# Expert units: the order of passes in the first part; first FFN group: the first product as three rounded products

## The chip, the cores and the metric

The kernel runs on one core of one Trainium2 chip. The metric is the device time of one execution in microseconds (us); the time of a kernel is the median of its runs. Engines are named as the profile names them: PE (TensorE matmul; PEld its weight loads), DVE (VectorE), ACT (ScalarE), POOL (GpSimd), SP (SyncE, whose queue issues most DMAs).

## What is computed

Three stages on 2304 tokens of width 512. A linear attention with 4 batches and 8 heads, an FFN with a softplus between its two products, and a routed layer in which each token goes to one of 8 experts:

```python
# attention: phi(x) = exp(x omega^T - |x|^2/2 - max) / sqrt(m)
num = einsum('bhsm,bhmd->bhsd', q_p, einsum('bhsm,bhsd->bhmd', k_p, v))
x = (num / (einsum('bhsm,bhm->bhs', q_p, k_p.sum(2)) + 1e-6))   # -> [2304, 512]
# FFN, d_ff = 2048
h = x @ w_in
x = (maximum(h, 0) + log1p(exp(-abs(h)))) @ w_out
# routed layer, 8 experts of hidden size 1024, one expert for each token
out[mask] = gate_w[mask, None] * (maximum(x[mask] @ w1[e], 0) @ w2[e])
```

The FFN's weights come from the host as 64-bit floats and are turned into 32-bit ones on the chip.

## The kernel before

**Formats of a product.** A product of two 32-bit operands is done in one of two ways. Plain: one matmul of type F32 for each block of 128 rows of the contraction; the profile shows it as two records on PE. Rounded: each operand is split into a high part (a copy rounded to the type F32R, `..h` or `..hi`) and a rest (the operand minus its high part, `..l` or `..lo`, F32R too); then three matmuls are summed: high by high, high by rest, rest by high. A split costs a cast (ACT, mostly) and a subtraction (DVE or POOL) for each operand.

**Attention** is cut into small steps (`stage_T`, `P`, `K`, `Z`, `Q`, `N`, `M`, `X`): transposes, projections (three matmuls `pp`, L282 to L284), the sums over keys (`kv`), the numerators and denominators (`nd`), and the division (`stage_M`, L425 and L426 on POOL, then a DVE operation at L433). `stage_X` splits the result into `xhi` (L252) and `xlo` (L444, on POOL). Of the first group of tokens it leaves out the split: L433 writes the plain tile `x` there.

**FFN.** Tokens go in 6 groups of 384 (`NG`), the hidden width in 16 chunks of 128 (`NF`). Chunk f of a group makes `h` (`mm1`, 128 by 384, contraction 512 in four blocks), the softplus (`r`, `t`, `gf` or `gh` and `gl`), and adds to the output sums `y` (`mm2`, L703). In group 0 both products are plain: four F32 matmuls on the chunk's weights `win` in `mm1` and three in `mm2`. In groups 1 to 5 they are rounded: `ring_in` casts the chunk's weights to `wih` (ACT, L597) and subtracts the rest `wil` (L598, DVE or POOL by the table `il`, in which the entries of group 0 are both POOL), in two buffers each, one chunk ahead.

During group 0 the FFN's weights are loaded and converted: 32 pieces (`w_in` and `w_out` of 16 chunks) pass through three staging buffers `wst`; SP issues the load, and three DVE operations make 32-bit floats of a piece (L558, L561, L564), after which its staging buffer is free for the next load.

The attention steps of later tokens are laid between the FFN's matmuls. Up to the first expert unit a scheduler sets the order of instructions on each engine; each engine then runs its own list in order.

**Expert units.** A unit is one block of 128 tokens of one expert (single, `slot_*`) or two (pair, `pair_*`). Four singles come first, then six times a pair and a single, then a last single. In these units, from the second on, the written order is kept. For each unit 2 MB of `w1` and 2 MB of `w2` are gathered by POOL's DMAs, cast on ACT (`w`, L1246) and their rests taken on DVE (L1250), `w1` in four blocks c = 0 to 3 while PE works on the unit ahead. The unit's first product is made in two parts (single, L1336, twelve matmuls of 128x512 each) or four (pair, L1358, 24 of 128x256 each). In each part the passes of one block stand together:

```python
PASSES = ((0, 0), (0, 1), (1, 0))        # (part of x, part of w1): 0 high, 1 rest
mms = [(xs[g][a][c], w1s[g, c][b_][:, w]) for c in range(NC) for a, b_ in PASSES]
```

Of the kernel before, what the change touches and what calls it, by code (L numbers as in the profile page):

```python
# [9 lines left out]
F32 = mybir.dt.float32  # L10
# [5 lines left out]
ALU = mybir.AluOpType  # L16
# [60 lines left out]
def tile_kernel(ctx, tc, q, k, v, omega, w_in, w_out, emb, tau, w1, w2, out):  # L77
# [156 lines left out]
    def x_tiles(g):  # L234
        if g == 0:

            xg[g] = xg.get(g) or [xpool.tile([P, NC, G], F32, tag="xhi", name="x_0"), None]
        elif g not in xg:
            xg[g] = [xpool.tile([P, NC, G], F32R, tag=f"x{s}", name=f"x{s}_{g}") for s in ("hi", "lo")]
        return xg[g]  # L240
# [174 lines left out]
    def stage_M(b, u, i, half):  # L415
# [10 lines left out]
        nc.gpsimd.tensor_tensor(out=den, in0=den, in1=rc, op=ALU.mult)  # L426

        parts = [(slice(0, HW[half]), xf)]
        if b == 0:
            parts = [(slice(o, o + n), x_tiles(0)[0][:, 2 * u + i, off:off + n] if g == 0 else xf[:, o:o + n])  # L430
                     for g, off, o, n in x_pieces(b, half)]
        for c, out_ in parts:
            nc.vector.scalar_tensor_tensor(out=out_, in0=den[:, c], scalar=2.0, in1=xf[:, c], op0=ALU.subtract,  # L433
                                           op1=ALU.mult, reverse0=True)

    def stage_X(b, u, i, half):
        den, xf = st.pop(("x", b, u, i, half))
        j = 2 * u + i
        for g, off, done, n in x_pieces(b, half):
            if g == 0:  # L440
                continue
            xh, xl = x_tiles(g)
            move("xh", b, u, xh[:, j, off:off + n], xf[:, done:done + n])
            eng("xl", b, u).tensor_tensor(out=xl[:, j, off:off + n], in0=xf[:, done:done + n],  # L444
                                          in1=xh[:, j, off:off + n].bitcast(F32), op=ALU.subtract)
# [135 lines left out]
    def conv_to(n):  # L581
        while done_w[0] < min(n, NW):
            next(conv, None)
# [5 lines left out]
    def ring_in(n):  # L589
        f = n % NF  # L590
        if n < NF:
            return
        assert done_w[0] >= 2 * f + 1
        ih = ring.tile([P, NC, P], F32R, tag="wih", name="wih")
# [26 lines left out]
    def mm1(n, rate):  # L621
        g, f = divmod(n, NF)
        xh, xl = xg[g]
        if g == 0:
            conv_to(2 * f + 1)
            passes = ((win_chunk(f), xh),)
        else:
            ih, il = wr.pop(("i", n))
            passes = ((ih, xh), (il, xh), (ih, xl))

# [25 lines left out]
        else:  # L656
            nc.vector.scalar_tensor_tensor(out=t, in0=r, scalar=2.0, in1=h[:, 0:G], op0=ALU.mult, op1=ALU.subtract)  # L657
        if n + 1 < NG * NF and n >= 1:
            ring_in(n + 1)
# [609 lines left out]
    PASSES = ((0, 0), (0, 1), (1, 0))  # L1269

    def unit_x(g):

# [55 lines left out]
    def slot_m1(g, half, part=slice(0, 12)):  # L1328
# [3 lines left out]
        w = slice(half * HF, half * HF + HF)  # L1332
        mms = [(xs[g][a][c], w1s[g, c][b_][:, w]) for c in range(NC) for a, b_ in PASSES]
        for i in range(part.start, part.stop):
# [16 lines left out]
    def pair_m1(g, k):  # L1351

        ph = hs["ps"] = mpsum("h", "ph")
        for c in range(NC):
            for j in range(2):
                f = slice(2 * k * P + j, 2 * (k + 1) * P, 2)
                for n, (a, b_) in enumerate(PASSES):
                    nc.tensor.matmul(ph[:, j * 256:j * 256 + 256], lhsT=w1s[g, c][b_][:, f],  # L1358
                                     rhs=xs[g][a][c].rearrange("p i t -> p (i t)"),
                                     start=(c == 0 and n == 0 and j == 0), stop=(c == NC - 1 and n == 2),  # L1360
                                     skip_group_check=True)

# [227 lines left out]
```

## Time and profile before

| | us |
|---|---|
| median of 3 runs | 950.11 (948.86 to 951.63) |
| the profiled execution's own time | 950.99 |
| its span, first to last instruction | 949.1 |
| PE busy over the span | 895.0 (94%) |
| DVE, ACT, POOL busy | 694.6, 651.7, 345.1 |
| granted TensorE clock, mean | 0.991 of full |

PE is busy nearly throughout, so the first thing to read is where it is not, and what its work costs from the start of one matmul to the start of the next: records of neighbouring matmuls overlap, so a group's mean duration is longer than what it takes of PE. The first 150 us, in which loads, conversions and attention share the engines with group 0, have to be read apart from the rest.

### The profile page before, as it was taken

What the parts mean: (1) busy time and instruction counts of PE and PEld (TensorE: products, weight loads), DVE (VectorE), ACT (ScalarE), POOL (GpSimd) and SP (SyncE); (2) the same over time, 40 slices, a digit from 0 to 9 for tenths busy, and PEclk for the clock granted to TensorE, in tenths of its full rate; (3) what the DMA queues carried; (4) which work ended last, traced back from release to release, by engine and by line L of the source; (5) the groups of instructions that cost most, each with busy time, mean ns of one, the idle gap of its engine ahead of it and who ended that gap; (6) DMA issues with size and microseconds to landing.
All of it is one profiled execution on the core that took longest, in us unless ns stands there. A gap on an engine that the chain in (4) does not pass through costs nothing. (4 is left out here: it accounts for less than half of the span.)

```text
span 949.1 us, 14505 instructions
## 1 busy us (share of the span) xinstructions
PE 895.0 (94%) x4951; PEld 743.6 (78%) x4951; DVE 694.6 (73%) x1376; ACT 651.7 (69%) x1452; POOL 345.1 (36%) x341
## 2 busy tenths in 40 slices
PE   7788989999999999999999999999999999999993
PEld 6666545588888879887888889887787887878872
DVE  6698875477888776689886777768967676685762
ACT  4787445477778867776777678876867576585672
POOL 1332400255446654566653110012653242252410
PEclk9999999999999999999999999999999999999997
DMA  4656660011262212010301281102114661451820
GB/s 117 188 170 199 185 180 28 12 39 37 56 147 69 48 47 71 26 40 17 67 7 23 73 331 63 34 12 57 34 56 161 253 240 70 169 211 36 324 86 6
DMA packets 86540, 94.69 MB, mean 100 GB/s; under 512 B 50294, under 2 KB 74870, under 8 KB 84160
## 3 DMA queue, kind: packets, MB, share of 16 engines
q1 hardware_dynamic: 77888, 45.21, 18.4%
q0 software_dynamic: 8576, 48.52, 13.7%
q8 instruction: 41, 0.67, 0.3%
q14 instruction: 35, 0.29, 0.1%
HBM read 108.36 MB, written 15.48 MB: 130 GB/s over the span
## 5 line engine op out<-in xcount | busy, mean ns | idle before, releaser
L1370 PE MATMUL po<-w,mh_h 128*128 128x512 f32 x368 | 116.8, 398 | 0.5 <-ACT mh_h L1347 0.5
L1385 POOL DMA_INDIRECT out_dram<-ot,s_idx x23 | 46.3, 2015 | 166.9 <-ACT ot L1384 126.0
L703 PE MATMUL y<-woh,gh 128*128 128x512 f32 x240 | 97.7, 411 | 3.2 <-DVE gh L682 3.2
L1250 DVE TENSOR_TENSOR w<-w2r,w 128x512 fp32r<-128x512 f32 x136 | 88.2, 687 | 12.3 <-ACT w L1246 12.1
L703 PE MATMUL y<-wol,gh 128*128 128x512 f32 x240 | 94.9, 398 | 0.0
L1246 ACT CAST w<-w2r 128x512 fp32r<-128x512 f32 x136 | 79.4, 643 | 18.4 <-DMA w2r<-in_moe_w_dram,w_idx 9.0
L1250 DVE TENSOR_TENSOR w<-w1r,w 128x1024 fp32r<-128x1024 f32 x68 | 80.3, 1226 | 11.2 <-ACT w L1246 11.2
L703 PE MATMUL y<-woh,gl 128*128 128x512 f32 x240 | 81.5, 406 | 0.4 <-POOL gl L683 0.4
L598 DVE TENSOR_TENSOR wil<-win,wih 128x512 fp32r<-128x512 f32 x72 | 56.9, 790 | 29.2 <-ACT wih L597 25.9
L638 PE MATMUL h<-xhi,wih 128*128 128x384 f32 x320 | 73.6, 349 | 2.8 <-DVE t L657 2.5
L1370 PEld LDWEIGHTS po<-w,mh_h 128*128 128x128 f32 x368 | 66.1, 189 | 12.2 <-ACT mh_h L1347 0.7
L1246 ACT CAST w<-w1r 128x1024 fp32r<-128x1024 f32 x68 | 71.9, 1121 | 3.8 <-PE ph L1336 2.1
L1358 PE MATMUL ph<-mxh,w 128*128 128x256 f32 x384 | 73.0, 286 | 1.4 <-DVE w L1250 0.5
L1370 PE MATMUL po<-w,mh_l 128*128 128x512 f32 x184 | 72.6, 395 | 1.7 <-DVE mh_l L1349 1.7
L425 POOL TENSOR_TENSOR xf<-xf,rc 128x256 f32<-128x256 f32 (+1 forms) x20 | 19.9, 994 | 143.7 <-ACT rc L424 129.0
L638 PE MATMUL h<-xlo,wih 128*128 128x384 f32 x320 | 71.9, 340 | 0.0
L638 PE MATMUL h<-xhi,wil 128*128 128x384 f32 x320 | 69.6, 337 | 0.0
L1358 PEld LDWEIGHTS ph<-mxh,w 128*128 128x128 f32 x384 | 62.7, 195 | 5.1 <-DVE w L1250 3.8
L610 POOL TENSOR_TENSOR wol<-wout,woh 128x512 fp32r<-128x512 f32 x40 | 54.2, 1355 | 27.8 <-ACT woh L609 24.9
L638 PEld LDWEIGHTS h<-xhi,wih 128*128 128x128 f32 x320 | 55.1, 188 | 7.6 <-DVE t L657 3.0
L638 PEld LDWEIGHTS h<-xhi,wil 128*128 128x128 f32 x320 | 57.5, 188 | 0.0
L638 PEld LDWEIGHTS h<-xlo,wih 128*128 128x128 f32 x320 | 56.5, 188 | 0.5
(311 smaller groups left out, 2415.1 us busy)
## 6 DMA issues: line engine op xcount, KB each, us to landing
wst<-in_moe_w_in_dram SPq DMA_DIRECT2D x16, 512.0 KB, 3.9
wst<-in_moe_w_out_dram SPq DMA_DIRECT2D x16, 512.0 KB, 3.7
raw<-in_k_dram SPq DMA_DIRECT2D x32, 128.0 KB, 2.3
vf<-in_v_dram SPq DMA_DIRECT2D x64, 64.0 KB, 2.2
raw<-in_q_dram SPq DMA_DIRECT2D x32, 128.0 KB, 2.3
ya<-yt SPq DMA_DIRECT2D x20, 128.2 KB, 3.9
yb<-yt SPq DMA_DIRECT2D x20, 128.2 KB, 3.6
ya<-yt SPq DMA_DIRECT2D x8, 256.5 KB, 4.7
```

The lines of the kernel that those rows point to most:

```text
L425: nc.gpsimd.tensor_tensor(out=xf, in0=xf, in1=rc, op=ALU.mult)
L598: feng("il", n).tensor_tensor(out=il, in0=wi, in1=ih.bitcast(F32), op=ALU.subtract)
L610: feng("ol", n).tensor_tensor(out=ol, in0=wo, in1=oh.bitcast(F32), op=ALU.subtract)
L638: nc.tensor.matmul(h[:, 0:G], lhsT=a[:, c, :], rhs=x[:, c, :], start=(i == 0), stop=(i == last))
L703: nc.tensor.matmul(y, lhsT=x[:, c], rhs=w, start=(f == 0 and i == 0), stop=(f == NF - 1 and i == len(passes) - 1))
L1246: nc.scalar.copy(out=hi, in_=src)
L1250: eng.tensor_tensor(out=lo, in0=src, in1=hi.bitcast(F32), op=ALU.subtract)
L1358: nc.tensor.matmul(ph[:, j * 256:j * 256 + 256], lhsT=w1s[g, c][b_][:, f], rhs=xs[g][a][c].rearrange("p i t -> p (i t)"), start=(c == 0 an ...
L1370: nc.tensor.matmul(po[s], lhsT=h[a][:, o:o + P], rhs=w2s[g, c][b_], start=(c == 0 and n == 0), stop=(c == 7 and n == 2))
L1385: nc.gpsimd.indirect_dma_start(out=out, out_offset=bass.IndirectOffsetOnAxis(ap=s_idx[:, s:s + 1].bitcast(U32), axis=0), in_=ot, in_offset ...
```

## The change

In group 0 the first product `mm1` is made rounded, as in the other groups: `x` of group 0 is split like the others' (`xhi`, `xlo`), `ring_in` runs for its 16 chunks too, and the single F32 pass over four blocks becomes three F32R passes. The order of the three passes in every group's `mm1` becomes high by high, weights' high by `x`'s rest, weights' rest by `x`'s high. `stage_M` writes its result with one DVE operation instead of one for each piece. In an expert unit's first part the matmuls with `w1`'s rests come after all the others (`first_order`); in a pair's parts the two halves j now alternate inside each pass.

```diff
--- before.py
+++ after.py
@@ -232,10 +232,7 @@
     xg = {}
 
     def x_tiles(g):
-        if g == 0:
-
-            xg[g] = xg.get(g) or [xpool.tile([P, NC, G], F32, tag="xhi", name="x_0"), None]
-        elif g not in xg:
+        if g not in xg:
             xg[g] = [xpool.tile([P, NC, G], F32R, tag=f"x{s}", name=f"x{s}_{g}") for s in ("hi", "lo")]
         return xg[g]
 
@@ -424,21 +421,12 @@
         nc.scalar.activation(out=rc, in_=rc, func=AF.Exp, scale=-1.0)
         nc.gpsimd.tensor_tensor(out=xf, in0=xf, in1=rc, op=ALU.mult)
         nc.gpsimd.tensor_tensor(out=den, in0=den, in1=rc, op=ALU.mult)
-
-        parts = [(slice(0, HW[half]), xf)]
-        if b == 0:
-            parts = [(slice(o, o + n), x_tiles(0)[0][:, 2 * u + i, off:off + n] if g == 0 else xf[:, o:o + n])
-                     for g, off, o, n in x_pieces(b, half)]
-        for c, out_ in parts:
-            nc.vector.scalar_tensor_tensor(out=out_, in0=den[:, c], scalar=2.0, in1=xf[:, c], op0=ALU.subtract,
-                                           op1=ALU.mult, reverse0=True)
+        nc.vector.scalar_tensor_tensor(out=xf, in0=den, scalar=2.0, in1=xf, op0=ALU.subtract, op1=ALU.mult, reverse0=True)
 
     def stage_X(b, u, i, half):
         den, xf = st.pop(("x", b, u, i, half))
         j = 2 * u + i
         for g, off, done, n in x_pieces(b, half):
-            if g == 0:
-                continue
             xh, xl = x_tiles(g)
             move("xh", b, u, xh[:, j, off:off + n], xf[:, done:done + n])
             eng("xl", b, u).tensor_tensor(out=xl[:, j, off:off + n], in0=xf[:, done:done + n],
@@ -589,8 +577,7 @@
     def ring_in(n):
         f = n % NF
         if n < NF:
-            return
-        assert done_w[0] >= 2 * f + 1
+            conv_to(2 * f + 1)
         ih = ring.tile([P, NC, P], F32R, tag="wih", name="wih")
         il = ring.tile([P, NC, P], F32R, tag="wil", name="wil")
         wi = win_chunk(f)
@@ -621,12 +608,10 @@
     def mm1(n, rate):
         g, f = divmod(n, NF)
         xh, xl = xg[g]
-        if g == 0:
-            conv_to(2 * f + 1)
-            passes = ((win_chunk(f), xh),)
-        else:
-            ih, il = wr.pop(("i", n))
-            passes = ((ih, xh), (il, xh), (ih, xl))
+        if ("i", n) not in wr:
+            ring_in(n)
+        ih, il = wr.pop(("i", n))
+        passes = ((ih, xh), (ih, xl), (il, xh))
 
         two = g >= LATE
         h = psa.tile([P, 512], F32, tag="pr", name="h") if two and n % 2 else \
@@ -655,7 +640,7 @@
             nc.scalar.activation(out=t, in_=h[:, 0:G], func=AF.Abs)
         else:
             nc.vector.scalar_tensor_tensor(out=t, in0=r, scalar=2.0, in1=h[:, 0:G], op0=ALU.mult, op1=ALU.subtract)
-        if n + 1 < NG * NF and n >= 1:
+        if n + 1 < NG * NF:
             ring_in(n + 1)
         nc.scalar.activation(out=t, in_=t, func=AF.Exp, scale=-1.0)
         nc.scalar.activation(out=t, in_=t, func=AF.Ln, bias=1.0)
@@ -1268,6 +1253,13 @@
     xs, w1s, w2s = {}, {}, {}
     PASSES = ((0, 0), (0, 1), (1, 0))
 
+    def first_order(part):
+
+
+        if part == 0:
+            return [(c, p) for c in range(NC) for p in ((0, 0), (1, 0))] + [(c, (0, 1)) for c in range(NC)]
+        return [(c, p) for c in range(NC) for p in PASSES]
+
     def unit_x(g):
 
         n = len(groups[g])
@@ -1330,7 +1322,7 @@
             hs["ps", half] = mpsum("h", "ph")
         ph = hs["ps", half]
         w = slice(half * HF, half * HF + HF)
-        mms = [(xs[g][a][c], w1s[g, c][b_][:, w]) for c in range(NC) for a, b_ in PASSES]
+        mms = [(xs[g][a][c], w1s[g, c][b_][:, w]) for c, (a, b_) in first_order(half)]
         for i in range(part.start, part.stop):
             x, r = mms[i]
             nc.tensor.matmul(ph, lhsT=x, rhs=r, start=(i == 0), stop=(i == 3 * NC - 1))
@@ -1351,14 +1343,13 @@
     def pair_m1(g, k):
 
         ph = hs["ps"] = mpsum("h", "ph")
-        for c in range(NC):
+        order = first_order(k)
+        for n, (c, (a, b_)) in enumerate(order):
             for j in range(2):
                 f = slice(2 * k * P + j, 2 * (k + 1) * P, 2)
-                for n, (a, b_) in enumerate(PASSES):
-                    nc.tensor.matmul(ph[:, j * 256:j * 256 + 256], lhsT=w1s[g, c][b_][:, f],
-                                     rhs=xs[g][a][c].rearrange("p i t -> p (i t)"),
-                                     start=(c == 0 and n == 0 and j == 0), stop=(c == NC - 1 and n == 2),
-                                     skip_group_check=True)
+                nc.tensor.matmul(ph[:, j * 256:j * 256 + 256], lhsT=w1s[g, c][b_][:, f],
+                                 rhs=xs[g][a][c].rearrange("p i t -> p (i t)"),
+                                 start=(n == 0 and j == 0), stop=(n == len(order) - 1), skip_group_check=True)
 
     def unit_m2(g, i, parts):
 
```

On DVE this is the place at which the conversion of the FFN's weights ends. `wout_...` is the last piece; its three operations are L558, L561 and L564 before, L546, L549 and L552 now; `t` is the softplus' argument of chunk 8 and `gf` its sum. Before:

```order
L558 TENSOR_SCALAR wout_2088<-wst 128x512
L561 SCALAR_TENSOR_TENSOR wout_2088<-wst,wout_2088 128x512
L657 SCALAR_TENSOR_TENSOR t<-r,h 128x384
L564 SCALAR_TENSOR_TENSOR wout_2088<-wst,wout_2088 128x512
L668 TENSOR_TENSOR gf<-r,t 128x384
```

Now:

```order
L642 SCALAR_TENSOR_TENSOR t<-r,h 128x384
L285 TENSOR_REDUCE nm<-pp 128x4
L546 TENSOR_SCALAR wout_2274<-wst 128x512
L549 SCALAR_TENSOR_TENSOR wout_2274<-wst,wout_2274 128x512
L293 TENSOR_TENSOR pe<-pp,nm 128x512
L653 TENSOR_TENSOR gf<-r,t 128x384
L552 SCALAR_TENSOR_TENSOR wout_2274<-wst,wout_2274 128x512
```

The last conversion stands at chunk 8 in both; now it comes behind `t` of that chunk, with two attention operations between.

On POOL, in the middle of group 0 (`xf` and `den` are the division, `xhi` and `xlo` the split of later groups' tokens). Before:

```order
L425 TENSOR_TENSOR xf<-xf,rc 128x256
L426 TENSOR_TENSOR den<-den,rc 128x256
L254 CAST xhi_589<-xf 128x192
L254 CAST xhi_1351<-xf 128x64
L444 TENSOR_TENSOR xlo_590<-xf,xhi_589 128x192
L444 TENSOR_TENSOR xlo_1352<-xf,xhi_1351 128x64
```

Now:

```order
L432 TENSOR_TENSOR xlo_594<-xf,xhi_593 128x192
L585 TENSOR_TENSOR wil<-win_1376,wih 128x512
L432 TENSOR_TENSOR xlo_1410<-xf,xhi_1409 128x64
L585 TENSOR_TENSOR wil<-win_1534,wih 128x512 x2
L585 TENSOR_TENSOR wil<-win_1723,wih 128x512 x2
L585 TENSOR_TENSOR wil<-win_1892,wih 128x512
L422 TENSOR_TENSOR xf<-xf,rc 128x256
```

The subtractions `wil` of group 0's chunks stand between POOL's other work.

On PE, the first part of a single that follows a pair (`w_c_0` is the high part of block c of `w1`, `w_c_1` its rest). Before:

```order
L1336 MATMUL ph<-w_0_0_8648,mx 128x512
L1336 MATMUL ph<-w_0_1_8649,mx 128x512
L1336 MATMUL ph<-w_0_0_8648,mx 128x512
L1336 MATMUL ph<-w_1_0_8652,mx 128x512
L1336 MATMUL ph<-w_1_1_8653,mx 128x512
L1336 MATMUL ph<-w_1_0_8652,mx 128x512
L1336 MATMUL ph<-w_2_0_8656,mx 128x512
L1336 MATMUL ph<-w_2_1_8657,mx 128x512
L1336 MATMUL ph<-w_2_0_8656,mx 128x512
L1336 MATMUL ph<-w_3_0_8660,mx 128x512
L1336 MATMUL ph<-w_3_1_8661,mx 128x512
L1336 MATMUL ph<-w_3_0_8660,mx 128x512
```

Now:

```order
L1328 MATMUL ph<-w_0_0_8853,mx 128x512 x2
L1328 MATMUL ph<-w_1_0_8857,mx 128x512 x2
L1328 MATMUL ph<-w_2_0_8861,mx 128x512 x2
L1328 MATMUL ph<-w_3_0_8865,mx 128x512 x2
L1328 MATMUL ph<-w_0_1_8854,mx 128x512
L1328 MATMUL ph<-w_1_1_8858,mx 128x512
L1328 MATMUL ph<-w_2_1_8862,mx 128x512
L1328 MATMUL ph<-w_3_1_8866,mx 128x512
```

The four matmuls on rests moved behind the eight on high parts.

## Rows read from the trace of the kernel before

**Rows 1.** The page's first part: busy time of each engine.

```profile
PE 895.0 (94%) x4951; PEld 743.6 (78%) x4951; DVE 694.6 (73%) x1376; ACT 651.7 (69%) x1452; POOL 345.1 (36%) x341
```

**Rows 2.** Busy time by stretch (PE, PEld, DVE, ACT, POOL), granted clock, DMA.

```profile
30.00:146.00 116.00, 99.73 (x497) 67.48 (x497) 98.55 (x206) 71.37 (x209) 31.86 (x33) 0.99 0.62 185
146.00:190.00 44.00, 44.00 (x158) 25.86 (x157) 20.68 (x40) 22.62 (x54) 7.96 (x12) 1.00 0.03 10
```

**Rows 3.** The timeline of PE: start, length, line, tiles, count, idle before.

```profile
145.66 2.85 PE L638 MATMUL h<-x,win 128*128 128x384 f32 x8 [0.87 <-DVE t L657]
...
170.99 2.75 PE L638 MATMUL h<-x,win 128*128 128x384 f32 x8
173.57 2.74 PE L703 MATMUL y<-wout,gf 128*128 128x512 f32 x6
...
196.30 0.94 PE L638 MATMUL h<-xhi,wih 128*128 128x384 f32 x4
...
198.47 0.39 PE L703 MATMUL y<-woh,gh 128*128 128x512 f32 x1
```

**Rows 4.** Groups by line and shape, whole span: count, busy, mean ns.

```profile
L597 ACT CAST wih<-win 128x512 fp32r<-128x512 f32 x80 | 49.5, 619 | 0.0
...
L598 POOL TENSOR_TENSOR wil<-win,wih 128x512 fp32r<-128x512 f32 x8 | 10.6, 1325 | 10.0 <-ACT wih L597 5.8 <-PE pp L284 3.5 <-PE pt_q L377 0.6
...
L444 POOL TENSOR_TENSOR xlo<-xf,xhi 128x256 fp32r<-128x256 f32 x4 | 3.6, 912 | 2.3 <-ACT xhi L252 2.3
...
L444 POOL TENSOR_TENSOR xlo<-xf,xhi 128x128 fp32r<-128x128 f32 x4 | 2.8, 694 | 4.5 <-ACT xhi L252 4.5
```

**Rows 5.** DVE's groups by line and shape, 30 to 146 us only.

```profile
L561 DVE SCALAR_TENSOR_TENSOR win<-wst,win 128x512 int32<-128x512 int32 x16 | 11.7, 732 | 0.1
...
L558 DVE TENSOR_SCALAR win<-wst 128x512 int32<-128x512 int32 x16 | 8.5, 534 | 6.3 <-DMA wst<-in_moe_w_in_dram 6.2
L558 DVE TENSOR_SCALAR wout<-wst 128x512 int32<-128x512 int32 x16 | 8.2, 511 | 8.3 <-DMA wst<-in_moe_w_out_dram 8.3
...
L598 DVE TENSOR_TENSOR wil<-win,wih 128x512 fp32r<-128x512 f32 x2 | 1.4, 680 | 0.0
```

**Rows 6.** Single lines: count, shortest, median and longest duration in ns.

```profile
L558 DVE TENSOR_SCALAR win<-wst x16: 414/427/1090, 35.2 to 141.3; 128x512 int32<-128x512 int32 x16
...
L561 DVE SCALAR_TENSOR_TENSOR win<-wst,win x16: 674/686/1381, 36.1 to 142.0; 128x512 int32<-128x512 int32 x16
```

**Rows 7.** The timeline of all engines, two lines near 76 us.

```profile
75.95 0.97 POOL L425 TENSOR_TENSOR xf<-xf,rc 128x320 f32<-128x320 f32 x1 [1.88 <-ACT rc L424]
76.09 1.38 DVE L561 SCALAR_TENSOR_TENSOR win<-wst,win 128x512 int32<-128x512 int32 x1
```

**Rows 8.** The same near 124 us.

```profile
123.41 0.43 DVE L558 TENSOR_SCALAR wout<-wst 128x512 int32<-128x512 int32 x1 [2.70 <-DMA wst<-in_moe_w_out_dram]
...
124.48 0.55 DVE L668 TENSOR_TENSOR gf<-r,t 128x384 f32<-128x384 f32 x1
...
125.09 0.70 PE L703 MATMUL y<-wout,gf 128*128 128x512 f32 x1 [1.69 <-DVE gf L668]
```

**Rows 9.** The same, first part of a single that follows a pair.

```profile
715.67 4.63 DVE L1250 TENSOR_TENSOR w<-w1r,w 128x1024 fp32r<-128x1024 f32 x4 [0.25 <-ACT w L1246]
...
716.67 1.24 PE L1336 MATMUL ph<-w,mx 128*128 128x512 f32 x4
...
718.09 0.98 PE L1336 MATMUL ph<-w,mx 128*128 128x512 f32 x3 [0.18 <-DVE w L1250]
...
720.36 1.90 PE L1336 MATMUL ph<-w,mx 128*128 128x512 f32 x7 [0.17 <-DVE w L1250]
```

**Rows 10.** The same, first part of a pair that follows a single.

```profile
730.45 3.55 DVE L1250 TENSOR_TENSOR w<-w1r,w 128x1024 fp32r<-128x1024 f32 x3 [0.26 <-ACT w L1246]
...
731.13 0.40 PE L1358 MATMUL ph<-mxh,w 128*128 128x256 f32 x2
...
734.05 0.39 PE L1358 MATMUL ph<-mxh,w 128*128 128x256 f32 x1 [0.16 <-DVE w L1250]
```

**Rows 11.** PE's waits over the span: us in total, times, longest.

```profile
PE ph L1336 <- DVE w L1250: 3.2, 19, 0.2
```

## The prediction

> **What bounds the kernel now.** I read the busy times first [rows 1]: PE works 94% of the span, so PE work that goes is worth its time wherever PE is the engine that everyone waits for, and nothing elsewhere. Which it is, the busy time by stretch tells [rows 2]. From 146 to 190 us PE is busy 44.00 of 44 us and DVE only 20.68: there PE is the bound. From 30 to 146 us PE has 99.73 of 116 us, but DVE has 98.55 busy, and [rows 5] show it idle another 6.3 and 8.3 us until a piece of FFN weights (`wst`) had landed. Together that is 113.2 of 116 us: up to the last conversion at 146 us the in-order list of DVE, with the loads in it, sets the pace. [Rows 8] show how PE comes to wait: DVE stands 2.70 us before a load, the sum `gf` of a chunk is queued behind, and PE's second product starts 1.69 us late. The change's FFN part thus falls into two stretches with different bounds: chunks 0 to 8 of group 0 before 146 us, chunks 9 to 15 after. Last I read the expert units [rows 9 to 11].
>
> **The product of group 0 on PE.** The plain product takes 173.57 - 170.99 = 2.58 us from its start to the next product's [rows 3]; the rounded one, as group 1 makes it, 198.47 - 196.30 = 2.17 us for its twelve matmuls. That is 0.41 us less for each chunk, 16 x 0.41 = 6.6 us of PE work. (The records' own lengths, 2.85 and 0.94 us, overlap and can't be used.) The rows of after 146 us carry 7 of these: 7 x 0.41 = 2.9 us, on the path. The other 3.7 us lie under DVE's list.
>
> **What it adds.** ACT: 16 casts of 0.619 us [rows 4], 9.9 us, and eight small ones for `x`. ACT is busy 71.37 of 116 and 22.62 of 44 us [rows 2], so the time is hidden; it would cost if a cast had to wait for its weights, since the `r` of the chunk ahead is queued behind it and PE's next product waits for that `r`. It doesn't: in the new order of DVE 20 of 32 pieces are converted when the sum of chunk 3 is made, so `w_in` is there up to chunk 9. POOL: up to the last conversion ten subtractions `wil` of 1.325 us and the rests of `x`, 4 x 0.912 and 4 x 0.694 us [rows 4], 13.3 + 6.4 = 19.7 us. POOL itself is busy 31.86 of 116 us, and the rest of a chunk is needed last, by the order of passes, so this too is hidden on POOL. The new split also stands ahead of the first product, up to 1.0 us; I take none of it, since DVE is the bound there.
>
> **What POOL does to DVE.** It is not hidden from DVE. In [rows 7] a conversion step starts 0.14 us after a POOL multiplication and takes 1.38 us, where the shortest of its kind takes 0.674 us [rows 6]; it ends 0.55 us after the POOL operation does, as if it had begun there. How much of POOL's time DVE loses on average is bounded by the conversion steps: L558 takes 534 ns in the mean [rows 5] and 414 at its shortest [rows 6], L561 732 and 674: 0.178 us for a piece of `w_in`, 2.85 us for 16, some 5.7 us with those of `w_out` taken alike, against POOL's 31.86 us [rows 2], or 0.18 us for each us of POOL. The third step and the sums meet POOL as well; I take 0.25, with 0.18 and 1 as the ends. So DVE gets 19.7 x 0.25 = 4.9 us more, and is spared two subtractions of 0.680 us [rows 5], which stood early as group 1's and now come after: net 3.5 us. Part of that fills the 14.6 us in which DVE waits for loads, part delays the next load, since a staging buffer is freed by DVE; I take half, 1.7 us later at the last conversion (ends: 0 and 3.5).
>
> The Trainium skill, "SBUF — State Buffer", section "SBUF: two separate sides", says that the port pair of VectorE and GpSimd is an exclusive lock: a GpSimd operation and a VectorE operation that reads two SBUF tensors, or runs in a two-port mode, shut each other out for a whole instruction. The single pair in [rows 7] agrees; the mean in [rows 5, 6] says how seldom they meet. If DVE lost all of POOL's time, by this rule, the sum below would be 14.7 + 1.9 = 16.6 us longer.
>
> **The sum for group 0.** At the last conversion both orders stand at chunk 8. After it PE is the bound: 1.7 us late, less 2.9 us. PE is also further on in the attention: 67 instead of 65 projections stand ahead of chunk 9's product, two times three matmuls of 256 columns, 0.12 us each if [rows 3] are scaled by columns (2.17 / 12 = 0.18 us for 384), 0.7 us. Together -1.9 us; ends -6.6 (all of PE's gain) and 19.7 - 1.4 - 2.9 - 0.7 = +14.7 (DVE loses all of POOL's time). The list for groups 1 to 5 is sorted anew as well, with the same operations; no row prices that, its sign is open, and I allow one wait like that of [rows 8], 2.7 us, either way in the range.
>
> **The expert units.** The visible idle time is small, 19 waits and 3.2 us [rows 11], but a matmul's record covers part of the gap behind it. By starts, in [rows 9]: four matmuls from 716.67 take 0.96 us (0.24 us each for 512 columns, scaled as above), the fifth starts at 718.09, 0.46 us late; six more from there take 1.44 of the 2.27 us to 720.36. The first part loses 1.3 us in all. The new order doesn't give that back, since the part can't end before the last block's rest is there: DVE makes the four rests from 715.67 in 4.63 us, to 720.30. Before, two matmuls of 0.24 us stood from there to the end of the part; now one. Gain 0.24 us. In the pair [rows 10] the rests are ready at 734.00; before, the 20th of 24 matmuls of 0.12 us began at 734.05 instead of 733.41, and five stood from there to the part's end; now the two on the last rest do: 0.36 us. The gain is 6 x 0.24 + 6 x 0.36 us, and 0.24 for the one early single that waits (19 = 6 x 3 + 1): 3.8 us. PE is back to back between such waits, so it stays. Ends: none, and 6 x 1.3 + 6 x 0.6 + 0.5 = 11.9 us, if DVE were early enough.
>
> **Sum.** -1.9 - 3.8 = -5.7 us. The profiled execution took 950.99 us, 1.9 more than its span and 0.9 more than the median of 950.11; so 945.3 us for it and 944.4 for a median.
>
> **Rivals.** *PE alone decides* (0.20): the waits for loads take up all that DVE loses, and what PE saves before 146 us pulls the loads and sums along. For it speaks that SP's loads wait in one queue with the attention's, which PE frees; against it DVE's 113.2 of 116 us. -6.6 - 3.8: 939.7 us. *The first group gives nothing* (0.22): the last conversion comes 3.6 us late and eats what chunks 9 to 15 save; only the expert units are left, 946.3 us, and where their gain goes too, 950.1. For it speaks that each conversion frees the buffer of a load that DVE waits for two pieces later. *POOL holds DVE back* (0.12), the slower side: in the list of DVE from 45 to 146 us, the added 19.7 us of POOL cost DVE a share p with nothing absorbed: 19.7 p - 1.4 - 2.9 - 0.7 - 3.8 us. It decides from p = 0.45; at 0.7 it is +5.0, 955.1 us. [Rows 7] show single operations that lose this much, the mean of [rows 5, 6] speaks against it.
>
> The skill's rule on the lock, named above, is this last rival's; taken at its word (p = 1) it gives +10.9 us, 961 us.
>
> **How the numbers follow.** The forecast has 0.46. The range goes from the first rival less 2.7 us, 937, to the second at its upper end plus 2.7, 953; the third is left out, and a little below. About 0.3% (2.9 us) is what a measurement of this kernel can tell from no change, so faster means under 947.3. Faster: 0.40 of the forecast's 0.46, the first rival's 0.20, 0.10 of the second: 0.70. Within: 0.06 + 0.12 = 0.18. Slower: 0.12.
>
> **What would show it.** In the profile of the changed kernel: twelve matmuls of group 0's product in 2.1 to 2.2 us; the last conversion between 145 and 150 us and group 1's first product 1 to 4 us earlier; L558 and L561 with means 50 to 100 ns higher; in a single's first part one wait ahead of the last rest in place of three, and the part's end 0.2 us nearer to DVE's last rest; a pair and a single together 0.6 us shorter. The forecast is wrong if the last conversion moves by over 4 us, if a wait for `wil` or `xlo` appears on PE, or if the part's end in [rows 9, 10] is not tied to DVE's last rest.

## The result and the profile after

The change made the kernel slower: 956.7 us in the median of four runs (953.92 to 957.71) against 950.65 us for the kernel before beside it. The recorded ratio is 1.0052 with a 95% interval of 1.0031 to 1.0073; the two medians by themselves give 1.0064. I had forecast 944.4 us, and 937 to 953 as the range. The profiled execution is the fastest of the four; its trace shows 3.0 us of the difference (span 952.1 against 949.1 us). Of the other three, 956.2 to 957.7 us, no trace is there; their granted clock was 0.981, that of the profiled one 0.987.

The busy times, which answer [rows 1]: PE has 6 us less to do, DVE 7 us more, POOL 14 us more.

```profile
PE 889.1 (93%) x5015; PEld 754.2 (79%) x5015; DVE 701.6 (74%) x1372; ACT 666.9 (70%) x1476; POOL 358.9 (38%) x365
```

Busy time by stretch, columns as in [rows 2]; the stretches end at the last conversion, at the last sum `gf` of group 0, at the first expert matmul and at the last expert matmul.

```profile
30.00:155.00 125.00, 102.40 (x561) 80.41 (x561) 111.39 (x209) 81.45 (x239) 52.20 (x55) 0.95 0.58 173
155.00:194.00 39.00, 39.00 (x177) 28.24 (x176) 21.57 (x38) 23.88 (x54) 13.06 (x15) 1.00 0.05 14
194.00:636.00 442.00, 429.01 (x2479) 376.24 (x2478) 332.66 (x683) 338.43 (x790) 193.98 (x187) 1.00 0.24 64
636.00:938.00 302.00, 295.45 (x1644) 249.07 (x1642) 214.94 (x398) 206.40 (x354) 93.37 (x72) 1.00 0.37 135
```

The same marks in both traces, in us:

| | before | after | difference |
|---|---|---|---|
| last conversion ends | 146.2 | 155.0 | +8.8 |
| ninth `gf` of group 0 starts | 146.7 | 153.8 | +7.1 |
| last `gf` of group 0 starts | 188.5 | 193.7 | +5.2 |
| from there to the first expert matmul (groups 1 to 5) | 439.9 | 442.0 | +2.1 |
| first to last expert matmul (the units) | 305.9 | 301.9 | -4.0 |

The ninth sum is the better measure of the delay: the last conversion stands behind the eighth sum before and behind the ninth after. So the units gave what the forecast had, most of the loss arose before 155 us, and groups 1 to 5 added 2.1 us. Up to 155 us DVE's groups have grown. First three of the groups of before that [rows 5] left out (30 to 146 us) and its sums, then the groups of after up to 155 us (count, busy us, mean ns, idle before; L546, L549 and L552 of after are L558, L561 and L564 of before, L653 is L668):

```profile
L561 DVE SCALAR_TENSOR_TENSOR wout<-wst,wout 128x512 int32<-128x512 int32 x16 | 11.5, 722 | 0.1
L564 DVE SCALAR_TENSOR_TENSOR win<-wst,win 128x512 int32<-128x512 int32 x16 | 11.3, 706 | 0.1
L564 DVE SCALAR_TENSOR_TENSOR wout<-wst,wout 128x512 int32<-128x512 int32 x16 | 11.0, 685 | 0.2
...
L668 DVE TENSOR_TENSOR gf<-r,t 128x384 f32<-128x384 f32 x8 | 4.4, 548 | 0.0
```

```profile
L549 DVE SCALAR_TENSOR_TENSOR win<-wst,win 128x512 int32<-128x512 int32 x16 | 14.5, 904 | 0.1
L549 DVE SCALAR_TENSOR_TENSOR wout<-wst,wout 128x512 int32<-128x512 int32 x16 | 13.8, 865 | 0.1
...
L552 DVE SCALAR_TENSOR_TENSOR win<-wst,win 128x512 int32<-128x512 int32 x16 | 13.0, 814 | 0.1
L552 DVE SCALAR_TENSOR_TENSOR wout<-wst,wout 128x512 int32<-128x512 int32 x16 | 10.9, 681 | 0.1
L546 DVE TENSOR_SCALAR wout<-wst 128x512 int32<-128x512 int32 x16 | 9.2, 573 | 3.8 <-DMA wst<-in_moe_w_out_dram 3.7
L546 DVE TENSOR_SCALAR win<-wst 128x512 int32<-128x512 int32 x16 | 7.8, 486 | 6.1 <-DMA wst<-in_moe_w_in_dram 6.0
L653 DVE TENSOR_TENSOR gf<-r,t 128x384 f32<-128x384 f32 x9 | 7.8, 867 | 1.0 <-ACT t L646 1.0
```

The same 96 conversion steps took 62.2 us before (with the rows of [rows 5]) and take 69.2 now, 7.0 more; nine sums at 867 in place of 548 ns are 2.9 more. POOL's busy time up to the last conversion rose by 52.20 - 31.86 = 20.3 us. DVE thus lost 9.9 us for 20.3 us of POOL, a share of 0.49. In all DVE was busy 111.39 - 98.55 = 12.8 us more up to the last conversion; the other 2.9 us are in the main operations that the new list puts ahead of it (one sum, two each of `nm`, `pe` and `den`, less two rests `wil`). Its idle time fell by 3.8 us, which leaves the 9 us of delay.

Whether it was POOL that made the steps longer, the records tell one by one. For each DVE operation from 30 us to the last conversion I take what it lasts over the shortest of its own form, and put that to the POOL operation that it overlaps longest. This comes to 7.7 us before and 19.0 after. Of the 19.0, 9.0 us stand beside the weights' rests (16.2 us of POOL, a share of 0.56), 1.9 beside the rests of `x` (11.6 us, 0.17), 7.1 beside POOL's other work, and 1.0 beside no POOL operation. So the time is lost beside POOL, and what the change added is nearly all beside the weights' rests.

How one such loss looks, on the timeline of DVE and POOL near 132 us:

```profile
131.85 0.43 DVE L546 TENSOR_SCALAR win<-wst 128x512 int32<-128x512 int32 x1 [0.73 <-DMA wst<-in_moe_w_in_dram]
131.96 1.44 POOL L585 TENSOR_TENSOR wil<-win,wih 128x512 fp32r<-128x512 f32 x1 [7.75 <-ACT wih L584]
132.19 1.76 DVE L552 SCALAR_TENSOR_TENSOR win<-wst,win 128x512 int32<-128x512 int32 x1
133.88 0.68 DVE L549 SCALAR_TENSOR_TENSOR win<-wst,win 128x512 int32<-128x512 int32 x1
```

The step at 132.19 ends at 133.95, 0.55 us after the subtraction, the figure of [rows 7]; the next one, with POOL idle, takes 0.68.

PE waits for the engine that lost: its three longest waits for DVE (us, times, longest; 30 to 160 us). No wait of PE's in group 0, these or a shorter one, is for `wil` or `xlo`: POOL's new work isn't late for PE, it makes DVE late.

```profile
PE pp L281 <- DVE xTlo L267: 4.2, 2, 3.2
PE pt_k L263 <- DVE xTlo L267: 3.0, 1, 3.0
PE pp L279 <- DVE pe L293: 2.6, 2, 2.1
```

### The profile page after: what moved, and what is told of

Same layout as the page of the kernel before. It is cut to its first block, busy times and chain, and to the rows that moved or that the text cites. A ratio compares the mean times of both kernels' runs of the same rounds, so it can differ in the third digit from the quotient of the medians.

```text
span 952.1 us, 14728 instructions
## 1 busy us (share of the span) xinstructions
PE 889.1 (93%) x5015; PEld 754.2 (79%) x5015; DVE 701.6 (74%) x1372; ACT 666.9 (70%) x1476; POOL 358.9 (38%) x365
## 5 line engine op out<-in xcount | busy, mean ns | idle before, releaser
L1376 POOL DMA_INDIRECT out_dram<-ot,s_idx x23 | 34.3, 1491 | 167.3 <-ACT ot L1375 137.1
L623 PE MATMUL h<-xhi,wih 128*128 128x384 f32 x384 | 89.5, 354 | 2.2 <-DVE t L642 1.0
L623 PE MATMUL h<-xlo,wih 128*128 128x384 f32 x384 | 85.9, 342 | 0.0
L623 PE MATMUL h<-xhi,wil 128*128 128x384 f32 x384 | 84.3, 339 | 0.0
L584 ACT CAST wih<-win 128x512 fp32r<-128x512 f32 x96 | 59.7, 622 | 23.9 <-PE h L623 23.1
L623 PEld LDWEIGHTS h<-xhi,wih 128*128 128x128 f32 x384 | 65.8, 189 | 11.6 <-DVE t L642 4.1
L623 PEld LDWEIGHTS h<-xlo,wih 128*128 128x128 f32 x384 | 69.7, 190 | 0.3
L623 PEld LDWEIGHTS h<-xhi,wil 128*128 128x128 f32 x384 | 68.6, 189 | 0.7
L1350 PE MATMUL ph<-mxh,w 128*128 128x256 f32 x384 | 62.7, 285 | 0.3
L285 DVE TENSOR_REDUCE nm<-pp 128x4 f32<-128x512 f32 (+1 forms) x80 | 50.3, 628 | 9.8 <-PE pp L281 9.6
```

Of the source, the lines that this page charges most:

```text
L285: nc.vector.tensor_reduce(out=nm[:, :2 * n], in_=ph, axis=AX.X, op=ALU.max, negate=True)
L584: nc.scalar.copy(out=ih, in_=wi)
L623: nc.tensor.matmul(h[:, 0:G], lhsT=a[:, c, :], rhs=x[:, c, :], start=(i == 0), stop=(i == last))
L1376: nc.gpsimd.indirect_dma_start(out=out, out_offset=bass.IndirectOffsetOnAxis(ap=s_idx[:, s:s + 1].bitcast(U32), axis=0), in_=ot, in_offset ...
```

## The experiments

For all kernels one table. POOL is its busy time from 30 us to the last conversion. "Six means" is the sum of the mean durations of the six conversion groups (L546, L549 and L552, or L558, L561 and L564, each for `win` and `wout`), in us, from 30 us to the last conversion. "Units" is the time from the first to the last expert matmul. All but the ratios are read from the one profiled execution of a kernel. How far one trace can be trusted, two pairs show whose kernels have the same lists up to the first expert matmul: the change and e1 have their last `gf` of group 0 at 193.7 and 191.7 us, e5 and e11 at 184.1 and 180.5. Smaller differences in group 0 tell nothing.

| kernel | ratio to before [95%] | POOL | six means | first expert matmul | units |
|---|---|---|---|---|---|
| before | 1 | 31.9 | 3.89 | 628.4 | 305.9 |
| the change | 1.0052 [1.0031, 1.0073] | 52.2 | 4.32 | 635.7 | 301.9 |
| e1 product only | 1.0077 [1.0053, 1.0101] | 53.6 | 4.40 | 635.4 | 305.3 |
| e2 units only | 0.9970 [0.9958, 0.9983] | 31.5 | 3.92 | 628.4 | 303.7 |
| e9 order of passes only | 1.0006 [0.9992, 1.0021] | 30.3 | 3.96 | 630.5 | 307.4 |
| e3 no weight rest | 0.9930 [0.9904, 0.9956] | 36.9 | 4.06 | 623.7 | 301.9 |
| e4 split unused | 1.0087 [1.0053, 1.0121] | 52.5 | 4.24 | 637.2 | 307.2 |
| e6 casts unused | 0.9972 [0.9951, 0.9993] | 29.7 | 3.81 | 626.1 | 306.9 |
| e7 32 memsets | 0.9984 [0.9968, 1.0001] | 44.7 | 3.96 | 629.0 | 307.2 |
| e12 48 memsets | 0.9998 [0.9983, 1.0013] | 54.5 | 3.89 | 628.2 | 307.0 |
| e5 rests on DVE | 0.9935 [0.9911, 0.9958] | 35.4 | 3.90 | 626.3 | 303.6 |
| e11 the same, old units | 0.9951 [0.9932, 0.9970] | 35.1 | 3.94 | 622.0 | 305.3 |
| e10 all rests on DVE | 0.9968 [0.9952, 0.9984] | 29.7 | 4.00 | 628.6 | 303.8 |
| e13 first half on DVE | 0.9898 [0.9874, 0.9922] | 41.5 | 4.09 | 625.4 | 303.5 |
| e14 second half on DVE | 0.9995 [0.9978, 1.0013] | 48.2 | 4.13 | 632.2 | 301.9 |

### The change taken apart

**e1**, the changed kernel with the units' old order:

```diff
-        mms = [(xs[g][a][c], w1s[g, c][b_][:, w]) for c, (a, b_) in first_order(half)]
+        mms = [(xs[g][a][c], w1s[g, c][b_][:, w]) for c in range(NC) for a, b_ in PASSES]
```

(and the pair's loop likewise; **e2** is the kernel before with the opposite edit, **e9** the kernel before with only this one:)

```diff
-            passes = ((ih, xh), (il, xh), (ih, xl))
+            passes = ((ih, xh), (ih, xl), (il, xh))
```

> The changed kernel with the expert units' old order of passes put back, so the group 0 part alone. In the traces the changed kernel is 7.3 us late at the first expert matmul (635.7 against 628.4) and 3.3 late at the last (937.6 against 934.3), so the units gained 4.0. Theory: the two parts add, and this one is about 4 us slower than the changed kernel's 956.7, some 960 to 961 (before 950.7), first expert matmul near 635.7, last near 941.6. Rival: the units' gain is only room left by the late start (their weights wait longer in SBUF), then this equals the changed kernel, 956 to 957.

> The kernel before with the new order of passes in the expert units alone. Theory: what the changed kernel gained between its first and last expert matmul is the order's own, 4.0 us: 946 to 947. Rival (the gain came from the late start of the units): 950 to 951, no difference.

> The kernel before with the order of the three passes of groups 1 to 5 changed as in the changed kernel (rest of the weights last), nothing else. It sorts the lists of groups 1 to 5 anew. In the changed kernel these groups took 442.0 us from the last sum of group 0 to the first expert matmul, before 439.9. Theory: such a sorting moves the time by a few us either way, 948 to 954. Rival: the pass order is itself worth something, more than 3 us faster.

The product alone is the whole loss: 956.84 us, by its ratio 0.77% above before. That is e1's rival's time, the change's own, and not the 960 to 961 us of its theory; its trace is the theory's (first expert matmul at 635.4, last at 940.7 us, 937.6 in the change). The intervals of the two ratios overlap, so the times alone don't show the units' gain inside the change. By themselves the units gain 0.30% (948.24 us, between the theory's 946 to 947 and the rival's 950), the order of passes nothing that can be measured. The first part of a single after, in answer to [rows 9] (DVE and PE on the timeline):

```profile
722.09 4.63 DVE L1235 TENSOR_TENSOR w<-w1r,w 128x1024 fp32r<-128x1024 f32 x4 [0.25 <-ACT w L1231]
...
723.10 1.65 PE L1328 MATMUL ph<-w,mx 128*128 128x512 f32 x6
...
724.96 1.43 PE L1328 MATMUL ph<-w,mx 128*128 128x512 f32 x5 [0.21 <-ACT w L1231]
...
726.78 0.50 PE L1328 MATMUL ph<-w,mx 128*128 128x512 f32 x1 [0.39 <-DVE w L1235]
```

DVE's rests end at 726.72, and only one matmul, at 726.78, stands behind them. By the starts (0.24 us a matmul, as in the prediction) the part now loses 0.42 us ahead of its seventh matmul and 0.62 ahead of its last, 1.04 in all, where before it lost 1.3. PE's waits in the units, for [rows 11], are fewer and longer:

```profile
PE ph L1328 <- DVE w L1235: 2.7, 7, 0.4
PE ph L1328 <- ACT w L1231: 1.3, 6, 0.2
```

### What POOL's subtractions cost

**e3**: the changed kernel without the weights' rests in group 0 (the third pass reads the high part once more, so that PE's work stays and one term of the product is left out); **e4**: the kernel before, with group 0's casts and rests made and used by nothing; **e6**: only the casts of these; **e7** and **e12**: the casts, and two or three memsets of the cast's tile on POOL, which read nothing.

```diff
# e3, to the changed kernel
...
-        feng("il", n).tensor_tensor(out=il, in0=wi, in1=ih.bitcast(F32), op=ALU.subtract)
+        if n >= NF:
+            feng("il", n).tensor_tensor(out=il, in0=wi, in1=ih.bitcast(F32), op=ALU.subtract)
+        else:
+            il = ih
# e4, to the kernel before; e6 leaves the subtraction out where n < NF
         if n < NF:
-            return
...
+            conv_to(2 * f + 1)
...
+            if n == 0:
+                ring_in(0)
...
-        if n + 1 < NG * NF and n >= 1:
+        if n + 1 < NG * NF:
             ring_in(n + 1)
# e7 (e12: range(3)), to e6
+        else:
+            for _ in range(2):
+                nc.gpsimd.memset(ih.bitcast(F32), 0.0)
```

> The changed kernel without the subtraction of the weights' rest in group 0; its third pass reads the high part once more, so that PE does the same matmuls (the rest is left out of group 0's first product). POOL loses 16 x 1.3 us. Theory, POOL's subtractions hold DVE's conversions back: the changed kernel's last conversion came at 155.0 instead of 146.2; of POOL's added time up to there about 13 us go, and with the share 0.54 us of DVE for each us of POOL that the two traces differ by, the last conversion comes near 148, and the kernel takes 949 to 951. Rival, the new order of the lists or the clock that fell in four stretches of the first 155 us: the conversion stays near 153 to 155 and the time near 955 to 957.

> The kernel before, with the 16 casts and 16 POOL subtractions of group 0's weights added and their results unused; the product stays plain, the units keep their order. Theory, POOL holds DVE back: the last conversion moves from 146.2 to 152 to 154, PE gains nothing after it, 956 to 958. Rival (the loss comes with the changed order of PE's matmuls and x's split, not from POOL): conversion near 147, 951 to 952.

> The kernel before with only the 16 casts of group 0's weights on ACT added, unused, no subtraction. With the subtractions as well it took 960.4 and the last conversion came at 153.5. Theory, the loss is POOL's: 950 to 952, conversion 146 to 148. Rival, the casts or the conversions asked for one chunk earlier do it: 956 to 960.

> As the run with the casts alone, but each cast's tile is then written twice by a POOL memset (about 0.6 us each, so as long as a subtraction, but reading nothing from SBUF). Theory, the lock is for SBUF reads on POOL against DVE operations with two SBUF inputs: little is lost, 950 to 953, and only the first conversion step (one input) gets longer. Rival, any POOL work in DVE's stretch costs the same: 956 to 960, as with the subtractions.

> The kernel before with group 0's 16 unused weight casts and three POOL memsets of each cast's tile, 48 of about 0.55 us, 26 us of POOL (the subtractions that nothing used were about 20 us and made 1.0087). Theory, it is POOL's reading of SBUF beside DVE's that costs: the memsets read nothing, ratio 0.998 to 1.002, DVE's L561 and L564 means as in the kernel before. Rival, it is POOL's time as such (its queue, and those who wait for POOL's attention work): ratio 1.009 or above.

Without the rests the changed kernel falls from 956.7 to 944.49 us, under the 949 to 951 that I expected, though its last conversion, at 150.3 us, came later than the 148. Its conversion steps stand ahead of the same sums as in the change, to within two; other operations stand elsewhere. Of the 12.0 us by which its first expert matmul is earlier, 6.8 arise in group 0 (last `gf` at 186.9 us) and 5.2 in groups 1 to 5, whose list is another. Put into the kernel before for nobody's use, the rests cost 0.87%; the casts alone cost nothing, they stand at 0.9972. So neither PE's new matmuls nor ACT's casts lost the time, but the 16 subtractions. And it is not POOL's time as such: e12 gives POOL more of it than e4 does (54.5 against 52.5 us), and its ratio is 0.9998. Against the casts alone, which all of these have, the subtractions cost 1.2%, the 48 memsets 0.3% and e7's 32 0.1%. e6, e7 and e12 run nearly the same lists; e4's is sorted otherwise, so that its time alone would leave the list as a rival. The records of e4 don't: by the count used above, 10.7 us of what its DVE operations last too long stand beside its subtractions (22.3 us of POOL, 0.48), in e12 2.4 beside the memsets (26.5 us, 0.09). Up to 146 us, e4 first (the lines of DVE are as in the kernel before):

```profile
L561 DVE SCALAR_TENSOR_TENSOR wout<-wst,wout 128x512 int32<-128x512 int32 x15 | 12.8, 856 | 0.1
L564 DVE SCALAR_TENSOR_TENSOR wout<-wst,wout 128x512 int32<-128x512 int32 x15 | 12.1, 804 | 0.1
...
L597 POOL TENSOR_TENSOR wil<-win,wih 128x512 fp32r<-128x512 f32 x14 | 19.5, 1399 | 33.5 <-ACT wih L596 32.7 <-DVE en_t L755 0.8
```

then e6:

```profile
L561 DVE SCALAR_TENSOR_TENSOR wout<-wst,wout 128x512 int32<-128x512 int32 x16 | 11.2, 701 | 0.2
L564 DVE SCALAR_TENSOR_TENSOR wout<-wst,wout 128x512 int32<-128x512 int32 x16 | 11.0, 684 | 0.2
```

and e12:

```profile
L561 DVE SCALAR_TENSOR_TENSOR wout<-wst,wout 128x512 int32<-128x512 int32 x15 | 11.3, 756 | 0.1
...
L564 DVE SCALAR_TENSOR_TENSOR wout<-wst,wout 128x512 int32<-128x512 int32 x15 | 10.3, 686 | 0.2
L558 DVE TENSOR_SCALAR wout<-wst 128x512 int32<-128x512 int32 x16 | 8.8, 549 | 6.0 <-DMA wst<-in_moe_w_out_dram 6.0
L558 DVE TENSOR_SCALAR win<-wst 128x512 int32<-128x512 int32 x16 | 8.3, 518 | 11.2 <-DMA wst<-in_moe_w_in_dram 11.1
...
L601 POOL MEMSET wih<- 128x512 f32 x46 | 25.2, 558 | 39.4 <-ACT wih L596 38.4
```

Against e6, the six means are 0.43 us longer in e4 (16 x 0.43 = 6.9 us for 52.5 - 29.7 = 22.8 us of POOL, 0.30) and 0.08 in e12 (1.3 us for 24.8, 0.05). What is left in e12 lies on the one-input step L558 (505 and 427 ns in e6); the two-input steps L561 and L564 are together no longer than in e6 (2.83 against 2.88 us).

The Trainium skill, "SBUF — State Buffer", section "SBUF: two separate sides", says just this: a VectorE operation with two SBUF inputs is shut out only by a GpSimd operation that reads SBUF. e4 against e12 agrees in kind (0.30 against 0.05), but DVE lost less than the whole of POOL's time.

### Where the rests should be made

**e5**, **e11**, **e10**, **e13** and **e14** move group 0's rests by the tables of the changed kernel (two letters of `il` for each group, first and second eight chunks; v is DVE, p POOL; e11 has the units' old order besides):

```diff
-    il='ppvpvvvvvvvv',
+    il='vvvpvvvvvvvv',      # e5, e11; e13: 'vpvp...', e14: 'pvvp...'
-    xl='pppppppp',
+    xl='vvpppppp',          # e10, beside e5's il
```

> The changed kernel with the weights' rests of group 0 made by DVE (one entry of the table il) instead of POOL. Theory, a POOL subtraction holds DVE back by about as long as it blocks: DVE now works 0.68 us itself where it lost about 0.54 x 1.33 = 0.7 us to POOL, so the last conversion stays at 153 to 156 and the time at 954 to 958. If a subtraction on POOL costs DVE more than that, conversion near 150 and 950 to 953. Rival, the loss is the wait for a late rest (POOL is slow), not DVE's time: the rest comes earlier, and the kernel falls under 950.

> The changed product of group 0 with its weight rests on DVE, and the units' passes in their old order. The new order alone took 0.3% off the kernel before, and with POOL's rests the product alone stood 0.25% above the whole change; if the two parts add up, the ratio is 0.996 to 0.997, so that the product with the rests on DVE is worth about 0.35% by itself. If the gain of the rests on DVE were one of a new sort of the units' loads, the ratio would be 1.000 or above.

> The changed kernel with group 0's weight rests on DVE, and now the activation rests of the first batch too (16 POOL subtractions xlo, 12.3 us of POOL before 150 us in the run with the weight rests on DVE alone, become 16 on DVE of about 0.35 us each, 5.6 us). Theory, POOL's reads hold DVE back by 0.54 us for each us of POOL: 6.6 us come back and 5.6 are paid, a ratio 0 to 3 us below that of the weight rests alone (0.990 to 0.994), and DVE's L549 and L552 means come down towards 700. Rival, the weight rests' gain was that POOL's queue, where a rest stood behind attention work, no longer made the product late: then there is nothing more to have, DVE only gets 5.6 us longer, ratio 0.997 to 1.000.

> The changed kernel with the weight rests of group 0's chunks 0 to 7 on DVE and of chunks 8 to 15 on POOL. Theory, what costs is POOL's subtractions while DVE still converts and is the bound: nearly all of them then lie in the chunks 0 to 8, so this kernel stands with the one that has all rests on DVE, ratio 0.992 to 0.996 (944 to 948 us), last product of group 0 before 187 us. Rival, each rest on POOL costs wherever it stands (eight of sixteen): half of the 1.2% between the two kernels, ratio 0.998 to 1.001.

> The changed kernel with the weight rests of group 0's chunks 0 to 7 on POOL, as in the changed kernel, and of chunks 8 to 15 on DVE. DVE's list begins as in the changed kernel: 30 of 64 conversion steps ahead of the first sum of a chunk, 54 ahead of the seventh. Theory, POOL's subtractions during the conversion cost: most of the loss stays, ratio 1.002 to 1.006, L549 with a mean of 850 to 900 ns up to the last conversion. Rival, each rest on POOL costs wherever it stands: 0.998 to 1.001. If it is 0.994 or lower, it was not POOL during the conversion that made the changed kernel slow.

e5 was a miss of mine: 946.45 us, not as slow as the change and under 950, as its rival had it. The rival's reason, a rest that comes late, is not in the trace of the change, where PE waits for no `wil`. The last conversion did stay late, at 154.5 us, but ten sums stand ahead of it, and the ninth starts at 142.1 us (153.8 in the change). The six means are back at 3.90, as before; DVE makes the rests itself and is no later than with POOL making them (busy 108.6 against 111.4 of 125 us). Its lists differ besides: in e5's 26 of 64 conversion operations L549 and L552 stand ahead of the first sum, as in the kernel before, in the changed kernel's 30. e10 was the next miss: moving the rests of `x` as well gave nothing back (six means 4.00) and put their time onto DVE, and the ratio is near its rival's 0.997. The share of 0.17 beside the rests of `x` in the change says the same: 0.5 is no price for every POOL operation. e11 says that the product with its rests on DVE is worth 0.49% alone; with the units' order it is 0.65%, less than the sum of the two.

e13 and e14 tell where the loss sits. Against the first expert matmul of the change at 635.7 us, e13 (first eight chunks' rests on DVE) is 10.3 us earlier and e14 (last eight) 3.5; e3, without any, 12.0; e14's 3.5 is no more than two traces of one list differ by (e5 and e11, 626.3 and 622.0). In e14 the last `gf` of group 0 starts at 194.1 us, as in the change (193.7); what it gains comes later, in groups 1 to 5 (438.1 us for 442.1). In e13 it starts at 185.1, in e3 at 186.9. So the loss in group 0 is that of the first eight chunks, those made while DVE converts. The ratio of e14, 0.9995, fell where the rival had it, because of that later part, which neither theory had, and its L549 took 837 and 803 ns, less than the 850 to 900 expected; e13 came out lower than either had it. How far PE is at 155 us shows in its groups; the changed kernel, 10 first products and 48 matmuls of the second,

```profile
L688 PE MATMUL y<-wout,gf 128*128 128x512 f32 x48 | 24.5, 640 | 2.0 <-DVE gf L653 1.8 <-DVE en_s L734 0.3
L623 PE MATMUL h<-xhi,wih 128*128 128x384 f32 x40 | 11.1, 394 | 0.1
```

and e13, 11 and 60, one chunk more of the first product and two of the second:

```profile
L688 PE MATMUL y<-wout,gf 128*128 128x512 f32 x60 | 29.5, 627 | 2.9 <-DVE gf L653 2.9
L623 PE MATMUL h<-xhi,wih 128*128 128x384 f32 x44 | 10.8, 364 | 2.2 <-DVE t L642 1.5 <-ACT xhi L249 0.6
```

e13 beats both kernels: 942.85 us (941.75 to 944.83, four runs), 1.0% under before; its interval and e5's overlap. Open is how much of e13's and e5's gain is the other order of DVE's list; e3 against the change leaves the conversion steps nearly where they were and shows that the rests are worth 5 to 7 us in group 0 (last `gf` at 186.9 us, against e1's 191.7 and the change's 193.7). Groups 1 to 5 take between 434.9 (e12) and 443.7 us (e1), and it is their list that moves them: kernels that share it lie within 1.6 us of each other (before and e2 at 439.8 and 439.7; the change and e1 at 442.1 and 443.7; e6, e7 and e12 at 436.3, 436.5 and 434.9; e5 and e11 at 442.2 and 441.5). Open is what makes one list better than another.

## Why the prediction was wrong

**The units: right in kind, the size with some luck.** -3.8 us forecast, -4.0 in the trace and 0.30% (2.9 us) by e2 alone. Traces that differ in this order only give less: 305.9 to 303.7 us (e2), 305.3 to 303.6 (e11 to e5), 305.3 to 301.9 (e1 to the change). A pair and a single are 0.57 us shorter in e2 (38.20 to 37.63 between POOL's writes of the output). One wait for ACT's cast and one for the last rest stand there in place of the three of [rows 9], the part's end is tied to DVE's last rest, as the step had it.

**The product on PE: right.** Twelve matmuls take 2.09 us (171.20 to 173.29), I had 2.17:

```profile
171.20 0.86 PE L623 MATMUL h<-xhi,wih 128*128 128x384 f32 x4
171.90 0.85 PE L623 MATMUL h<-xlo,wih 128*128 128x384 f32 x4
172.59 0.86 PE L623 MATMUL h<-xhi,wil 128*128 128x384 f32 x4
173.29 2.74 PE L688 MATMUL y<-wout,gf 128*128 128x512 f32 x6
```

**What is gained behind the last conversion: too much.** From the last conversion to the last sum it is 3.6 us less, as the sum's 2.9 + 0.7, but by luck: the lists don't stand at the same sum there, as the prediction took it. From the ninth sum to the sixteenth it is 41.8 us before and 39.8 after, 1.9 gained; the rest of the 3.6 is that the ninth sum now stands ahead of the last conversion.

**What POOL does to DVE: the step that failed.** The added POOL time was right, 20.3 us for 19.7. Its share was taken as 0.25, from the mean over POOL's work of before; for the added work it is 0.49, so that DVE lost 9.9 us and not 4.9. For the rests of `x` a mean like that would have done (0.17 by the records); the weights' rests cost 0.56. Nor does the mean of [rows 5, 6] say how seldom the two meet, as the prediction reads it: all of POOL's 33 operations up to the last conversion of before ran beside one of DVE's. Why a weights' rest costs DVE more than an older operation of the same length is not shown. The half that the waits for loads should take up was too much as well: DVE was busy 12.8 us more, and its idle time fell by 3.8 (its waits for loads by 4.8, 14.5 to 9.7, while a new one of 1.0 for ACT came in). The last conversion came 8.8 us late, where the forecast had 1.7 and called itself wrong from 4. Of the means, forecast 50 to 100 ns higher, L561's rose by 172 and 143 ns and L558's by -48 and 62.

**The rival that came nearest** was the one that POOL holds DVE back, with a chance of 0.12, and it decides from p = 0.45, as I had written. Its own formula gives only +0.9 us at 0.49. The marks give 8.8 - 3.6 + 2.1 - 4.0 = 3.3 us: what the formula lacks is mainly the 2.1 us of groups 1 to 5, sorted anew, which I had kept in the range only; the rest is 0.5 us more at the last conversion, less 0.2 in the units. At the Trainium skill's word (p = 1) it would have been 961 us; about half of that share was measured.

## What to carry to other kernels

Where DVE is saturated, count a subtraction on GpSimd as work of DVE too: by the count of the records the weights' rests cost it a third to somewhat over a half of their time here (0.33 in e13, 0.36 in e14, 0.48 in e4, 0.56 in the change), and the forecast, from older work, had a quarter. The kernels that made those rests on DVE itself, all of them or only those of the saturated stretch, were faster here, with another order of DVE's list. Judge the price of added work by the rows in the place where it will stand. Work moved off PE gains only in the stretches where PE is late; here 6.6 us of it was less than what preparing it cost.

## What the hardware showed beside

After some stretches in which PE worked little, the granted clock fell to its lower level for a while. In the changed kernel, from 125 to 155 us in steps of 5 (columns as in [rows 2]):

```profile
125.00:130.00 5.00, 2.97 (x19) 2.49 (x17) 4.94 (x12) 0.21 (x1) 0.00 (x0) 1.00 0.64 202
130.00:135.00 5.00, 4.90 (x10) 2.21 (x11) 4.23 (x7) 3.79 (x11) 1.44 (x1) 0.66 0.13 39
...
145.00:150.00 5.00, 3.06 (x8) 1.23 (x8) 4.53 (x8) 1.27 (x3) 1.50 (x1) 1.00 0.49 165
150.00:155.00 5.00, 4.16 (x17) 4.07 (x17) 4.80 (x9) 3.24 (x9) 1.88 (x2) 0.67 0.10 31
```

PE is busy 2.97 and 3.06 of 5 us, and in the next 5 us a mean of 0.66 and 0.67 of 2.4 GHz is granted, so that a part of them ran at 1.2 GHz. In the kernel before the same stretch has 1.00 throughout, and so has its stretch from 45 to 55 us, where PE is busy 3.02 and 3.47 of 5 us. Up to the last conversion the mean is 0.95 in place of 0.99, by my estimate (125 x 0.05 - 116 x 0.01) some 5 us of full clock. It is not settled what part of the 8.8 us that is. A low mean there doesn't by itself go with a slow kernel: e12 has a mean of 0.96 up to there and a ratio of 0.9998, e14 0.92 and 0.9995; and e4's slowest run, 961.28 us, had a granted clock of 0.990 over the whole.
